# First mixture of a fused attention and two-mixture kernel: blocks of 256 tokens, rows fetched one expert ahead, gate weight kept in the row

## The chip, the cores and the metric

The kernel runs on one core of a Trainium2 chip. Its engines are TensorE (PE in the rows, PEld its weight loads, PEq and PEldq its sequencer), VectorE (DVE), ScalarE (ACT), GpSimd (POOL) and SyncE (SP, which here only issues transfers). Each engine runs its own instruction stream in order. The metric is the device time in microseconds; lower is better.

## The reference

```python
# attention: (B,H,S,D) = (4,8,576,64), softmax inside chunks of 64; then x = (2304, 512)
def _moe_ref(x, w_gate, w1, w2, capacity):        # first mixture: one expert per token
    logits = x @ w_gate                            # E = 8
    expert_idx = np.argmax(logits, axis=1)
    gate_w = softmax(logits)[arange(N), expert_idx]
    # the first `capacity` = 576 tokens of each expert are kept, in order of token
    h = np.maximum(disp[e] @ w1[e], 0.0)           # (tokens, 512) @ (512, 1024)
    y = h @ w2[e]                                  # (tokens, 1024) @ (1024, 512)
    out[i] = gate_w[i] * y[...] if kept else 0
def _moe2_ref(x, w_gate, w1, w2):                  # second mixture: every expert for every token
    P = exp(logits - max); 8 rounds of row and column normalisation
    out = sum over e of P[:, e] * (relu(x @ w1[e]) @ w2[e])
```

All matrix products of the mixtures are made in three fp16 products (high x high, high x low, low x high) that accumulate in PSUM.

## The kernel before

There are three stages. The first does attention and the routing, tile by tile of 128 tokens. It leaves in HBM the token rows `xs_d` (high and low fp16 halves side by side, 2 KB a row), their gate weights `kx_d` (one word a row), and on the chip the table `gidx`, which lists the tokens of each expert in groups of 128, and the counts `reg_i`. The second stage, the first mixture, is the one that changes. The third is the second mixture over all tokens, three quarters of the span.

The first mixture goes through the eight experts in a Python loop. `rc` is the expert's token count, loaded into a register of every engine (line 760), `rb` its first row in the output. `gather` (line 642) issues two indirect transfers on POOL, for the rows and for the gate weights. `turn` (line 653) transposes the rows by a transfer that SP issues. `block` (line 673) computes 128 tokens: the first layer of 8 x 12 matmuls of 128 columns (line 685) into PSUM in two groups of four, each group cut into a high half by ACT (line 688) and a low half by DVE (line 689); the second layer of 24 matmuls of 512 columns (line 697); scaling; and two writes by SP, of the rows (line 709) and of coefficient and token (line 715). Block 0 of an expert is always computed, its rows being fetched one expert ahead. Blocks 1 to 3 stand each under `tc.If(rc > 128 * t)` (line 807), which also fetches the next tile; a loop for whatever lies beyond four blocks stands under `tc.If(rc > 512)` (line 812) inside the last one. An engine whose branch is not taken jumps over the block's instructions.

The same engines prepare the weights two experts ahead. Every expert has 4 MB of fp32 weights, loaded by SP in pieces of 512 KB (`loads`, in `parts`, between the blocks). `w_stat` takes statistics (ACT for the first matrix, DVE for the second), `w_scale` reduces them over the partitions on POOL, and `w_split` rounds to a high half on ACT (line 212) and leaves a low half on DVE (line 213), in eight steps. These steps are run at `sites` between the parts of a block: 5 and 7 after the two groups of block 0, and the others in blocks 1 to 3, or in an `Else` where those are skipped. For the last matrix (the seventh expert prepares the first of the second mixture) the splits are replaced by twelve steps of `w_quad` (line 220): for each quarter POOL makes four sums into the one buffer `wsum`, and ACT and DVE round them (lines 237 and 238).

Before the first block, `rows0` is gathered straight away, the loads of the third expert's weights are issued, the second expert's weights are split, and `turn_first` transposes the first tile on TensorE (line 667).

Of the kernel before, what the change touches and what calls it, by code (L numbers as in the profile page):

```python
# [10 lines left out]
F16 = mybir.dt.float16  # L11
# [18 lines left out]
def kernel(ctx, tc, q, k, v, w_gate, w1, w2, capacity, w2_gate, w21, w22, out):  # L30
# [11 lines left out]
    NSTAT = 4  # L42
# [10 lines left out]
    xs_d = dram.tile([N, DM], F32, name="xs_d")  # L53
    kx_d = dram.tile([N, 1], F32, name="kx_d")
# [19 lines left out]
    def pow2_of_max(mx, n, log2, tag):  # L74
        m, s, inv = smw(tag + "m", [128, n]), smw(tag + "s", [128, n]), smw(tag + "i", [128, n])
# [90 lines left out]
    def w_scale(x, nm):  # L166
        m = mats[x, nm]
        if x > E:
            m.am = over_partitions(m.mx, {"a": 288, "b": 292}[nm], 4)
            return  # L170
        m.am = smw("wam" + nm, [128, 4])
        op = bass.bass_isa.ReduceOp.add if m.ssq else bass.bass_isa.ReduceOp.max
        nc.gpsimd.partition_all_reduce(out_ap=m.am, in_ap=m.mx, channels=128, reduce_op=op)

    def w_scale2(x, nm):
        m = mats[x, nm]
        mm = smw("wmm" + nm, [128, 1])
        nc.vector.tensor_reduce(out=mm, in_=m.am, axis=AX.X, op=ALU.add if m.ssq else ALU.max)
        if m.ssq:
            m.s, m.inv = smw("ws" + nm, [128, 1]), smw("wi" + nm, [128, 1])  # L180
            pow2_of_sumsq(mm, LF, small.tile([128, 1], I32, tag="wh", name="wh"), m.s, m.inv)
        else:
            m.s, m.inv = pow2_of_max(mm, 1, LW, "w" + nm)
        other = mats.get((x, {"a": "b", "b": "a"}[nm]))
        if hasattr(other, "inv"):
            iw = iws[x] = smw("iw", [128, 1])
            nc.vector.tensor_tensor(out=iw, in0=other.inv, in1=m.inv, op=ALU.mult)


    def w_slot(x, n):  # L190
        pool, tag = slots.get(x, (wpool, 4 * (x % 3 // 2))) if x < E else (wpool, 0)
        return pool.tile([128, 4096], F16, tag=f"s{tag + n}", name=f"w{x}_{n}")

# [65 lines left out]
    with ExitStack() as actx:  # L259
# [145 lines left out]
        def st_lo(i):  # L405
# [3 lines left out]
            (nc.gpsimd if i < NT - 3 else nc.sync).dma_start(out=xs_d[i * 128:(i + 1) * 128, :], in_=hl.bitcast(F32))  # L409
# [23 lines left out]
        def route(g):  # L433
# [109 lines left out]
            def r_out():  # L543
                nc.vector.tensor_tensor(out=t["kx"], in0=t["kx"], in1=GT[g]["inv"], op=ALU.mult)
                (nc.gpsimd if g < NG - 1 else nc.sync).dma_start(out=kx_d[g * G * 128:(g + 1) * G * 128, :].rearrange("(j p) o -> p (j o)", p=128), in_=t["kx"])
# [84 lines left out]
    with ExitStack() as cctx:  # L630
# [5 lines left out]
        first = wpool.tile([128, 4096], F16, tag="s7", name="first")  # L636
# [5 lines left out]
        def gather(idx, tag, xg=None):  # L642
            if xg is None:
                xg = cp.tile([128, DM], F32, tag="xg" + tag, name="xg")
# [5 lines left out]
            return idx, kg, xg  # L650


        def turn(pre, tag):
            idx, kg, xg = pre
            xT = cp.tile([128, 2 * KD, 128], F16, tag="xT" + tag, name="xT")
            nc.sync.dma_start_transpose(out=xT, in_=xg.bitcast(F16))
            return idx, kg, xT

        def gather_t(idx, tag):
            return turn(gather(idx, tag), tag)  # L660

        def turn_first(pre):
            idx, kg, xg = pre
            xT = first[:, 1024:2048].rearrange("p (k n) -> p k n", n=128)
            p = ps_c.tile([128, 2 * KD, 128], F16, tag="y1", name="p_t")
            for kk in range(2 * KD):
                nc.tensor.transpose(p[:, kk, :], xg.bitcast(F16)[:, kk * 128:(kk + 1) * 128], id16)
            nc.scalar.copy(out=xT[:, 0:KD], in_=p[:, 0:KD])
            nc.vector.tensor_copy(xT[:, KD:2 * KD], p[:, KD:2 * KD])
            return idx, kg, xT  # L670


        def block(x, pre, row0, tag, sites=((), (), ())):
            a, b = mats[x, "a"], mats[x, "b"]
            idx, kg, xT = pre
            hh = cp.tile([128, KF, 128], F16, tag="hh" + tag, name="hh", bufs=1)
            hl = cp.tile([128, KF, 128], F16, tag="hl" + tag, name="hl", bufs=1)
            for fg in range(KF // 4):
                p = ps_c.tile([128, 4, 128], F32, tag="p" + tag, name="p_h")
                for f4 in range(4):  # L680
                    f = fg * 4 + f4
                    n = 0
                    for w, lo in ((a.hi, 0), (a.hi, KD), (a.lo, 0)):
                        for kk in range(KD):
                            nc.tensor.matmul(p[:, f4, :], lhsT=w[:, kk, f * 128:(f + 1) * 128], rhs=xT[:, lo + kk, :],  # L685
                                             start=(n == 0), stop=(n == 3 * KD - 1))
                            n += 1
                nc.scalar.activation(out=hh[:, fg * 4:fg * 4 + 4, :], in_=p, func=AF.Relu)  # L688
                nc.vector.scalar_tensor_tensor(out=hl[:, fg * 4:fg * 4 + 4, :], in0=p, scalar=0.0,  # L689
                                               in1=hh[:, fg * 4:fg * 4 + 4, :], op0=ALU.max, op1=ALU.subtract)  # L690
                for f in sites[fg]:
                    f()
            y = ps_c.tile([128, DM], F32, tag="y" + tag, name="p_y")
            n = 0
            for kk in range(KF):
                for h, w in ((hh, b.hi), (hh, b.lo), (hl, b.hi)):
                    nc.tensor.matmul(y, lhsT=h[:, kk, :], rhs=w[:, kk, :], start=(n == 0), stop=(n == 3 * KF - 1))  # L697
                    n += 1
            sq, ssq = cp.tile([128, DM], BF16, tag="sq" + tag, name="sq2", bufs=1), sm("ssq2" + tag, [128, 1])
            nc.scalar.activation(out=sq, in_=y, func=AF.Square, accum_out=ssq)  # L700
            s, inv = sm("x2s" + tag, [128, 1]), sm("x2i" + tag, [128, 1])
            pow2_of_sumsq(ssq, LX, sm("x2h" + tag, [128, 1], I32), s, inv)

            rhl = cp.tile([128, 2, 2, DM // 2], F16, tag="row" + tag, name="row2", bufs=1)
            yh = y.rearrange("p (c n) -> p c n", c=2)
            nc.scalar.activation(out=rhl[:, :, 0, :], in_=yh, func=AF.Copy, scale=s)
            nc.vector.scalar_tensor_tensor(out=rhl[:, :, 1, :], in0=yh, scalar=s, in1=rhl[:, :, 0, :],
                                           op0=ALU.mult, op1=ALU.subtract)
            nc.sync.dma_start(out=x2_d[bass.ds(row0, 128), :],
                              in_=rhl.rearrange("p c l n -> p (c l n)").bitcast(F32))  # L710
            to = sm("rkt" + tag, [128, 2])
            nc.gpsimd.tensor_copy(to[:, 1:2].bitcast(I32), idx)
            nc.vector.scalar_tensor_tensor(out=to[:, 0:1], in0=kg, scalar=inv, in1=iws[x],
                                           op0=ALU.mult, op1=ALU.mult)
# [475 lines left out]
```

## Time and profile before

| | us |
|---|---|
| median of 3 runs | 1937.91 (1935.62 to 1939.22) |
| the profiled execution | 1938.3 |
| its span, first to last instruction | 1936.6 |
| TensorE busy in the span | 1780.1 |
| mean granted TensorE clock | 0.96 of full speed |

The profile's times are microseconds from the span's start. Busy time is the union of an engine's instructions; matmuls overlap, so the mean of one is longer than its share of the time. In a row of the timeline the two first numbers are start and length, `xN` counts merged instructions, and the bracket gives the idle time of that engine before them and what ended it.

### The profile page before, as it was taken

To read this page: it belongs to the slowest core of one execution; us is meant where nothing else is said; L and a number is where in the kernel's file an instruction comes from. 1 tells how busy PE (TensorE), PEld (TensorE's weight loads), DVE (VectorE), ACT (ScalarE), POOL (GpSimd) and SP (SyncE) were. 2 spreads that over 40 slices of the span, in tenths; PEclk is the share of its full clock that TensorE was granted. 3 is DMA by queue.
4 is the path that set the end of the run, shared out by engine and by line. 5 is a ranking of instruction groups with operands and counts; after the bars stand their busy time and mean duration, and the time that the engine had idled before them with its cause. 6 is when DMAs were issued, how large, how long until landed. Compare 5 with 4: busy or idle time off the path is not lost.

```text
span 1936.6 us, 28661 instructions
## 1 busy us (share of the span) xinstructions
PE 1780.1 (92%) x11303; PEld 1022.2 (53%) x11303; DVE 1016.2 (52%) x1960; ACT 708.9 (37%) x1283; POOL 429.0 (22%) x504
## 2 busy tenths in 40 slices
PE   7864868767999899999999999999999999999997
PEld 5753556545554445555555555555555555555553
DVE  5886465563656663464445345544545553465432
ACT  7954354453433333343323224312333332242210
POOL 1252021232110321041122113210311231042221
PEclk9976889888999899999999999999999999999999
DMA  9974666764414120222121121302311211211210
GB/s 224 189 155 132 178 178 146 156 162 91 139 66 128 58 96 6 101 80 79 58 78 67 58 94 64 101 18 84 101 58 58 101 44 57 101 58 63 78 39 33
DMA packets 146523, 182.91 MB, mean 94 GB/s; under 512 B 74352, under 2 KB 92784, under 8 KB 146352
## 3 DMA queue, kind: packets, MB, share of 16 engines
q1 hardware_dynamic: 139584, 165.09, 30.0%
q0 software_dynamic: 5712, 15.49, 2.9%
q8 instruction: 109, 1.79, 0.4%
q14 instruction: 62, 0.51, 0.1%
q10 hardware_dynamic: 1056, 0.03, 0.0%
HBM read 147.52 MB, written 22.97 MB: 88 GB/s over the span
## 4 chain that ended last, share of the span: by engine, by line
PE 67%; DVE 4%; ACT 3%; issue 1%; POOL 1%; DMA 0%; POOLq 0%; DVEq 0%
PE p_m L1075 38%; PE p_m L1013 28%; DVE c L1019 1%; DVE el L1030 1%; ACT eh L1029 1%; ACT wsq L154 1%; POOL w L1048 1%; PE p_m L903 0%; PE p_l L163 0%; ACT m L1038 0%; ACT m L1058 0%; DVE w L213 0%; DVE u L1019 0%; ACT w L212 0%; DMA out_dram<-acc,rk 0%
## 5 line engine op out<-in xcount | busy, mean ns | idle before, releaser
L1075 PE MATMUL p_m<-w,eh 128*128 128x512 f16 x2304 | 685.4, 379 | 0.6 <-ACT eh L1029 0.6
L1013 PE MATMUL p_m<-x,w 128*128 128x384 f16 x4032 | 667.7, 327 | 1.3 <-DVE c L1019 1.3
L1013 PEld LDWEIGHTS <-w 128*128 128x128 f16 x4032 | 396.2, 99 | 265.0 <-issue 6.8
L1075 PE MATMUL p_m<-w,el 128*128 128x512 f16 x1152 | 436.6, 379 | 0.0
L1075 PEld LDWEIGHTS <-eh 128*128 128x128 f16 x2304 | 225.4, 98 | 267.8 <-ACT eh L1029 1.1
L1029 ACT ACTIVATE eh<-c 128x384 f16<-128x384 f32 x384 | 190.5, 518 | 413.4 <-DVE c L1019 413.2
L1048 POOL TENSOR_TENSOR w<-u,m 128x384 f32<-128x384 f32 x96 | 96.6, 1006 | 991.0 <-DVE u L1019 913.5
L1147 DVE SCALAR_TENSOR_TENSOR acc<-p_m,cf,acc 128x512 f32<-128x512 f32 x126 | 94.6, 751 | 383.2 <-PE p_m L1075 377.0
L1030 DVE SCALAR_TENSOR_TENSOR el<-c,eh 128x384 f16<-128x384 f32 x384 | 217.9, 569 | 127.0 <-ACT eh L1029 116.5
L1038 ACT COPY m<-p_m 128x384 f32<-128x384 f32 x96 | 44.6, 465 | 399.6 <-PE p_m L1013 399.6
L1075 PEld LDWEIGHTS <-el 128*128 128x128 f16 x1152 | 112.7, 98 | 136.5 <-DVE el L1030 0.8
L685 PE MATMUL p_h<-xT,w 128*128 128x128 f16 x1824 | 125.7, 239 | 55.6 <-PEq L807 26.4
L685 PEld LDWEIGHTS <-w 128*128 128x128 f16 x1920 | 130.9, 110 | 64.3 <-issue 48.6
L697 PE MATMUL p_y<-w,hh 128*128 128x512 f16 x320 | 98.3, 390 | 7.3 <-ACT hh L688 7.3
L1053 POOL TENSOR_TENSOR c<-u,m 128x384 f32<-128x384 f32 x96 | 95.7, 997 | 3.6 <-DVE u L1019 3.1
L1019 DVE TENSOR_TENSOR u<-p_m,m 128x384 f32<-128x384 f32 x96 | 53.4, 556 | 61.7 <-PE p_m L1013 61.7
L1019 DVE TENSOR_TENSOR c<-p_m,w 128x384 f32<-128x384 f32 x96 | 53.5, 557 | 49.4 <-PE p_m L1013 33.5
L237 ACT ACTIVATE w<-wsum,wsa 128x1024 f16<-128x1024 f32 x32 | 36.6, 1145 | 90.1 <-POOL wsum L231 90.1
L1019 DVE TENSOR_TENSOR u<-p_m,u 128x384 f32<-128x384 f32 x96 | 53.5, 557 | 28.7 <-PE p_m L1013 26.8
L154 ACT ACTIVATE wsq<-sta 128x1024 bf16<-128x1024 f32 x64 | 67.5, 1054 | 0.6
L238 DVE SCALAR_TENSOR_TENSOR w<-wsum,wsa,w 128x1024 f16<-128x1024 f32 x32 | 41.1, 1283 | 46.8 <-ACT w L237 46.8
L697 PE MATMUL p_y<-w,hl 128*128 128x512 f16 x160 | 62.6, 391 | 2.7 <-DVE hl L689 2.7
(226 smaller groups left out, 1564.8 us busy)
## 6 DMA issues: line engine op xcount, KB each, us to landing
x<-xt_d SPq DMA_DIRECT2D x147, 384.0 KB, 4.5
sta<-in_moe_w_dram SPq DMA_DIRECT2D x18, 1024.0 KB, 7.0
stb<-in_moe_w_dram SPq DMA_DIRECT2D x18, 1024.0 KB, 7.6
sta<-in_moe_w_dram SPq DMA_DIRECT2D x28, 512.0 KB, 7.7
stb<-in_moe_w_dram SPq DMA_DIRECT2D x28, 512.0 KB, 8.5
xt_d<-x SPq DMA_DIRECT2D x21, 384.0 KB, 2.9
x_d<-row SPq DMA_DIRECT2D x20, 256.0 KB, 4.8
vbd<-in_v_dram SPq DMA_DIRECT2D x72, 64.0 KB, 4.5
```

Source lines behind the costliest of these rows:

```text
L154: nc.scalar.activation(out=sq, in_=src, func=AF.Square, accum_out=m.mx[:, h:h + 1])
L685: nc.tensor.matmul(p[:, f4, :], lhsT=w[:, kk, f * 128:(f + 1) * 128], rhs=xT[:, lo + kk, :], start=(n == 0), stop=(n == 3 * KD - 1))
L697: nc.tensor.matmul(y, lhsT=h[:, kk, :], rhs=w[:, kk, :], start=(n == 0), stop=(n == 3 * KF - 1))
L1013: nc.tensor.matmul(p, lhsT=wt[:, w, lw, kk, :], rhs=xt[:, lx, kk, :], start=(n == 0), stop=(n == 5))
L1019: nc.vector.tensor_tensor(out=c, in0=p, in1=t, op=ALU.add)
L1029: nc.scalar.activation(out=hh[:, sl], in_=src, func=AF.Relu)
L1030: nc.vector.scalar_tensor_tensor(out=hl[:, sl], in0=src, scalar=0.0, in1=hh[:, sl], op0=ALU.max, op1=ALU.subtract)
L1038: nc.scalar.copy(out=Q["m1"], in_=p)
L1048: nc.gpsimd.tensor_tensor(out=Q["w"], in0=Q["u2"], in1=Q["m5"], op=ALU.add)
L1053: nc.gpsimd.tensor_tensor(out=Q["c22"], in0=Q["u3"], in1=Q["m5"], op=ALU.add)
L1075: nc.tensor.matmul(y, lhsT=h[:, t * 128:(t + 1) * 128], rhs=w[:, kk, :], start=(n == 0), stop=(n == 3 * KF - 1))
L1147: nc.vector.scalar_tensor_tensor(out=acc[:, j, :], in0=y, scalar=coefs[x][:, j:j + 1], in1=acc[:, j, :], op0=ALU.mult, op1=ALU.add)
```

## The change

1. `xs_d` is made 8 words wider (520 words a row). The gate weight is written eight times over into these words, and `kx_d` goes; so one gather brings rows and gate weight, and `weights` copies the weight out of the gathered row on POOL.
2. `blocks` computes one or two tiles of 128 tokens in one first layer: the matmuls take 256 columns, PSUM groups hold two or four of the eight column blocks, in four buffers. The second layer still goes by tile.
3. An expert is now at most two such calls and the loop: tiles 0 and 1 under `tc.If(rc > 128)`, with an `Else` that computes tile 0 alone, then tiles 2 and 3 under `tc.If(rc > 256)` and `tc.If(rc > 384)`, with an `Else` for tile 2 alone. Tile 0 is no longer outside of the branches.
4. `fetch` gathers and transposes two tiles. Tiles 2 and 3 of an expert are fetched when the expert begins, tiles 0 and 1 of the next expert right after them, whether they hold tokens or not, and outside of the branches.
5. The steps of weight preparation go, all of them, into the first call (2, 2, 1 and 7 after the four groups, 5 after tile 0, the rest after tile 1; 3, 7 and the rest in the `Else`). The loads stand after the first and after the second call. At the stage's start the transposes of tiles 2 and 3 stand before the loads of the third expert.

```diff
+    XW = DM + 8
+    xs_d = dram.tile([N, XW], F32, name="xs_d")
-            (nc.gpsimd if i < NT - 3 else nc.sync).dma_start(out=xs_d[i * 128:(i + 1) * 128, :], in_=hl.bitcast(F32))
+            (nc.gpsimd if i < NT - 3 else nc.sync).dma_start(out=xs_d[i * 128:(i + 1) * 128, 0:DM], in_=hl.bitcast(F32))
...
+                wide = lambda a: a.unsqueeze(2).to_broadcast([128, G, XW - DM])
+                nc.vector.tensor_tensor(out=t["kx"], in0=wide(kx), in1=wide(GT[g]["inv"]), op=ALU.mult)
+                (nc.gpsimd if g < NG - 1 else nc.sync).dma_start(out=xs_d[g * G * 128:(g + 1) * G * 128, DM:XW].rearrange("(j p) o -> p j o", p=128), in_=t["kx"])
...
+        def gather(idx):
+            xg = cp.tile([128, XW], F32, tag="xg", name="xg", bufs=4)
             nc.gpsimd.indirect_dma_start(out=xg, out_offset=None, in_=xs_d[:, :],
                                          in_offset=bass.IndirectOffsetOnAxis(ap=idx, axis=0))
-            kg = cp.tile([128, 1], F32, tag="kg" + tag, name="kg", bufs=4)
-            nc.gpsimd.indirect_dma_start(out=kg, out_offset=None, in_=kx_d[:, :],
-                                         in_offset=bass.IndirectOffsetOnAxis(ap=idx, axis=0))
+            return idx, xg[:, DM:DM + 1], xg
+        def fetch(idxs, tag, bufs):
+            xT = cp.tile([128, 2 * KD, 128 * len(idxs)], F16, tag="xT" + tag, name="xT", bufs=bufs)
+            rows = []
+            for n, (idx, kg, xg) in enumerate([gather(idx) for idx in idxs]):
+                nc.sync.dma_start_transpose(out=xT[:, :, n * 128:(n + 1) * 128], in_=xg[:, 0:DM].bitcast(F16))
+                rows.append((idx, kg))
+            return xT, rows
+        def weights(pre):
+            xT, rows = pre
+            for n, (idx, kx) in enumerate(rows):
+                kg = cp.tile([128, 1], F32, tag="kg", name="kg", bufs=6)
+                nc.gpsimd.tensor_copy(kg, kx)
...
+        def blocks(x, pre, nb, row0, sites=()):
+            W = 128 * nb
+            FG = 512 // W
+            for fg in range(KF // FG):
+                p = ps_c.tile([128, FG, W], F32, tag="p", name="p_h", bufs=4)
+                for f4 in range(FG):
+                    for w, lo in ((a.hi, 0), (a.hi, KD), (a.lo, 0)):
+                        for kk in range(KD):
+                            nc.tensor.matmul(p[:, f4, :], lhsT=w[:, kk, f * 128:(f + 1) * 128], rhs=xT[:, lo + kk, 0:W],
...
+                site()
+            for t in range(nb):
+                y = ps_c.tile([128, DM], F32, tag="y", name="p_y", bufs=3)
...
+        rows0 = [gather(gidx[:, 0, t:t + 1]) for t in (0, 1)]
+        late = fetch([gidx[:, 0, t:t + 1] for t in (2, 3)], "c", 1)
...
+            cur = weights(pre)
+            if x > 0:
+                late = fetch([gidx[:, x, t:t + 1] for t in (2, 3)], "c", 1)
             if x + 1 < E:
+                pre = fetch([gidx[:, x + 1, t:t + 1] for t in (0, 1)], "m", 2)
...
+            with tc.If(rc > 128) as cmp:
+                blocks(x, cur, 2, rows(0), spread((2, 2, 1, 7, 5)))
+            with cmp.Else():
+                blocks(x, cur, 1, rows(0), spread((3, 7)))
+            for f in (loads(3, "a", 0, 4) if x == 0 else []) + (loads(x + 3, "b", 0, 4) if x != E - 3 else []):
+                f()
+            weights(late)
+            with tc.If(rc > 256):
+                with tc.If(rc > 384) as cmp:
+                    blocks(x, late, 2, rows(2))
+                    with tc.If(rc > 512):
+                        with tc.For_i(4, (rc + 127) // 128, 1) as t:
+                            idx = cp.tile([128, 1], I32, tag="idx", name="idx")
+                            nc.vector.tensor_copy(idx, gidx[:, x, bass.ds(t, 1)])
+                            blocks(x, weights(fetch([idx], "l", 1)), 1, lambda _: rank(t))
+                with cmp.Else():
+                    blocks(x, late, 1, rows(2))
+            for f in loads(E, "b", 0, 4) if x == E - 3 else loads(x + 4, "a", 0, 4):
+                f()
```

## Rows read from the trace of the kernel before

**Rows 1.** The page: busy time by engine, share of the span, instructions.

```profile
PE 1780.1 (92%) x11303; PEld 1022.2 (53%) x11303; DVE 1016.2 (52%) x1960; ACT 708.9 (37%) x1283; POOL 429.0 (22%) x504
```

**Rows 2.** The first mixture as one window: length, busy time of each engine, clock, DMA.

```profile
core 0: us, PE busy (x) PEld busy (x) DVE busy (x) ACT busy (x) POOL busy (x), PEclk, DMA share, GB/s
...
166.90:473.80 306.90, 241.08 (x2400) 176.77 (x2399) 173.64 (x313) 147.28 (x225) 75.84 (x102) 0.87 0.64 154
```

**Rows 3.** Windows of the eight experts, second-layer matmuls (line 697) alone.

```profile
166.90:228.50 61.60, 23.94 (x96) 9.65 (x96) 0.85 0.55 148
228.50:249.90 21.40, 5.34 (x24) 2.31 (x24) 0.85 0.55 167
249.90:308.00 58.10, 21.37 (x96) 9.24 (x96) 0.88 0.76 174
308.00:348.00 40.00, 16.03 (x72) 6.93 (x72) 0.96 0.65 158
348.00:381.20 33.20, 10.69 (x48) 4.62 (x48) 0.88 0.79 167
381.20:405.40 24.20, 5.34 (x24) 2.31 (x24) 0.71 0.89 199
405.40:450.50 45.10, 18.49 (x72) 7.17 (x72) 0.87 0.45 104
450.50:473.80 23.30, 10.69 (x48) 4.62 (x48) 0.93 0.54 138
```

**Rows 4.** TensorE's timeline, first expert: starts of two layers and the next.

```profile
212.35 0.59 PE L697 MATMUL p_y<-w,hh 128*128 128x512 f16 x2
...
217.53 5.52 PE L685 MATMUL p_h<-xT,w 128*128 128x128 f16 x96
222.89 0.59 PE L697 MATMUL p_y<-w,hh 128*128 128x512 f16 x2
```

**Rows 5.** TensorE's timeline, layers that began after idle time.

```profile
231.99 6.64 PE L685 MATMUL p_h<-xT,w 128*128 128x128 f16 x87 [2.33 <-issue]
...
250.26 3.25 PE L685 MATMUL p_h<-xT,w 128*128 128x128 f16 x29 [6.44 <-PEq L807]
258.82 6.28 PE L685 MATMUL p_h<-xT,w 128*128 128x128 f16 x67 [5.31 <-issue]
...
363.67 8.36 PE L685 MATMUL p_h<-xT,w 128*128 128x128 f16 x96 [4.67 <-DMA xT<-xg]
...
430.60 0.61 PE L697 MATMUL p_y<-w,hh 128*128 128x512 f16 x2 [3.92 <-ACT hh L688]
```

**Rows 6.** Waits from 160 to 482 us: total, times, longest.

```profile
PE p_h L685 <- PEq L807: 26.4, 5, 11.0
...
PE p_h L685 <- DMA xT<-xg: 14.7, 4, 6.6
```

**Rows 7.** Branches on TensorE's queue (min/median/max ns): two lines, then 243 to 252 us.

```profile
L807 PEldq COMPARE_BRANCH  x34: 73/178/5293, 183.6 to 473.9; - x34
...
L812 PEldq COMPARE_BRANCH  x4: 176/258/343, 224.5 to 307.7; - x4
...
L807 PEldq COMPARE_BRANCH  x2: 822/2748/4674, 244.0 to 245.0; - x2
```

**Rows 8.** Timeline of all engines at the start of the first mixture.

```profile
152.95 1.76 SPq L143 DMA_DIRECT2D sta<-in_moe_w_dram  x4
...
159.15 0.96 POOL L648 DMA_INDIRECT kg<-kx_d,gidx  x1 [4.35 <-DMA kx_d<-gkx]
165.26 1.03 PE L667 MATMUL p_t<-id,first 128*128 128x128 f16 x8 [15.73 <-DMA first<-xs_d,gidx]
```

**Rows 9.** Groups by shape in the first mixture: busy us, mean ns, idle before.

```profile
L685 PEld LDWEIGHTS <-w 128*128 128x128 f16 x1919 | 130.7, 110 | 64.3 <-issue 48.6 <-DMA xT<-xg 6.2 <-DVE w L213 4.7
...
L238 DVE SCALAR_TENSOR_TENSOR w<-wsum,wsa,w 128x1024 f16<-128x1024 f32 x4 | 5.1, 1281 | 10.8 <-ACT w L237 10.8
...
L230 POOL TENSOR_TENSOR wsum<-sta 128x256 f32<-128x256 f32 x4 | 2.9, 720 | 0.0
```

**Rows 10.** The page's DMA issues: median us from issue to landing.

```profile
xT<-xg SPq DMA_TRANSPOSE x25, 7.1
```

More of the change, by code (lines that the diff above doesn't have):

```diff
@@ L41 @@
     scale = 1.0 / math.sqrt(D)
-    NSTAT = 4
     G = 3
@@ L653, in turn @@
[L653 to L670, printed above, removed]
@@ new lines, in turn_first @@
+        def turn_first(pres):
+            xT = cp.tile([128, 2 * KD, 256], F16, tag="xTm", name="xT", bufs=2)
+            for n, (idx, kg, xg) in enumerate(pres):
+                p = ps_c.tile([128, 2 * KD, 128], F16, tag="y", name="p_t", bufs=3)
+                for kk in range(2 * KD):
+                    nc.tensor.transpose(p[:, kk, :], xg[:, 0:DM].bitcast(F16)[:, kk * 128:(kk + 1) * 128], id16)
+                sl = slice(n * 128, (n + 1) * 128)
+                nc.scalar.copy(out=xT[:, 0:KD, sl], in_=p[:, 0:KD])
+                nc.vector.tensor_copy(xT[:, KD:2 * KD, sl], p[:, KD:2 * KD])
+            return xT, [(idx, kg) for idx, kg, _ in pres]
@@ new lines, in blocks, with site @@
+        def blocks(x, pre, nb, row0, sites=()):
+            a, b = mats[x, "a"], mats[x, "b"]
+            xT, rows = pre
+            W = 128 * nb
+            sites = list(sites)
+            def site():
+                for f in (sites.pop(0) if sites else ()):
+                    f()
+            hh = cp.tile([128, KF, 256], F16, tag="hh", name="hh", bufs=1)[:, :, 0:W]
+            hl = cp.tile([128, KF, 256], F16, tag="hl", name="hl", bufs=1)[:, :, 0:W]
+            FG = 512 // W
+            for fg in range(KF // FG):
+                p = ps_c.tile([128, FG, W], F32, tag="p", name="p_h", bufs=4)
+                for f4 in range(FG):
+                    f = fg * FG + f4
@@ L689, in block @@
[L689 to L714, printed above, removed]
@@ L719, in each @@
+            while sites:
+                site()
         def each(f, x, nm, n, *args):
@@ L762 @@
             y = x + 2
+            steps = []
+            if y <= E:
+                for nm in "ab":
+                    w_keep(y, nm)
             if y < E:
@@ L798, in rank, with rows @@
                                           skip_runtime_bounds_check_because="a block starts before the last token")
-            def rest(lo):
-                with tc.For_i(lo, (rc + 127) // 128, 1) as t:
-                    idx = cp.tile([128, 1], I32, tag="idx", name="idx")
-                    nc.vector.tensor_copy(idx, gidx[:, x, bass.ds(t, 1)])
-                    block(x, gather_t(idx, "1"), rank(t), "1")
-            for t in range(1, NSTAT):
-                with tc.If(rc > 128 * t) as cmp:
-                    if t + 1 < NSTAT:
-                        pre[t + 1] = gather_t(gidx[:, x, t + 1:t + 2], "1")
-                    block(x, pre[t], rank(t), "1", sites[t])
-                    if t + 1 == NSTAT:
-                        with tc.If(rc > 128 * NSTAT):
-                            rest(NSTAT)
-                            if x == E - 1:
-                                heads()
-                if any(sites[t]):
-                    with cmp.Else():
-                        for fs in sites[t]:
-                            for f in fs:
-                                f()
-                for f in parts[2 * t + 1]:
-                    f()
+            def rows(t0):
+                return lambda t: rb if t0 + t == 0 else rank(t0 + t)
```

114 lines of the change are left out of this document (59 added, 55 removed).

## The prediction, made before the changed kernel was run

> **What bounds the kernel now.** I read the page's busy line first, to see whether TensorE is the limit: 1780.1 of 1936.6 us busy [rows 1]. That average hides one stage. Cut by stretches, the first mixture runs from 166.9 to 473.8 us, 306.9 us, with TensorE busy 241.1 and a granted clock of 0.87, between its two levels of 1.2 and 2.4 GHz [rows 2]; what follows, 1936.6 - 473.8 = 1462.8 us, the change does not touch. Third, the stretches of the eight experts: 24 second-layer matmuls are one block, so the rows show 4, 1, 4, 3, 2, 1, 3 and 2 blocks, 20 in all [rows 3]. Fourth, TensorE's timeline, for what a block costs when nothing waits: the second layer from 212.35 to 217.53, 5.18 us; the first layer's 96 matmuls from 217.53 to 222.89, 5.36 us, 55.8 ns each [rows 4]. So 20 blocks are 20 x 10.54 = 210.8 us of work, and 306.9 - 210.8 = 96.1 us are lost. By expert, length less blocks x 10.54: 19.4, 10.9, 15.9, 8.4, 12.1, 13.7, 13.5, 2.2. This is all there is to win.
>
> Fifth, what the losses are. The first layer waits 14.7 us in four places for the transposed rows, and 26.4 us in five for TensorE's sequencer at the `If` of line 807 [rows 6]. Nothing computes there: the sequencer is at a branch. Of the 34 branches at that line the middle one takes 178 ns and the longest 5293 ns; those of line 812, which jump over one block, at most 343 ns; after the second expert, where three bodies are skipped in a row, two took 822 and 4674 ns [rows 7]. So a jump over one block is cheap, one that goes further can cost 4 to 5 us, and TensorE then waits again inside its matmuls, for nothing that the profile shows: 2.33 us after 9 matmuls, 5.31 us after 29 [rows 5]. Idle time costs twice. After 4.67 us of it the next first layer takes 8.36 us where the full pace takes 5.52 [rows 4, 5]: 2.8 us more.
>
> **Wider matmuls.** Eight pairs (2+2+1+1+1+1) and four single blocks replace 20 blocks. A first layer of 128 columns already runs at 128/2.4 = 53.3 ns plus 2.5, with the weight load hidden; 256 columns are then 106.7 + 2.5 = 109.2 ns, 10.5 us a pair against 10.7. Eight pairs save 2 us, so the work is 208.6 us. The Trainium skill (TensorE: Matmul & The Clock Gate, section Back-to-back issue gap) gives about 81 ns as the sustained distance of such pairs of load and matmul at 128 columns. The trace disagrees: 55.8 ns. By the page the 768 weight loads that fall away would be worth some 25 ns each, an estimate of 19 us more.
>
> **Rows outside the branches.** The four waits for transposes, 14.7 us [rows 6], and the slow matmuls after them are in no term of the sum below: I take them as gone, since each transpose is now issued at least one pair, 21 us, before its use. But three of the tiles that waited are the first after a pair, and there a new branch stands instead.
>
> **Branches.** This is the dear part. Before, a skipped tile is one `If`; TensorE jumps 1, 3, 1, 1, 2, 3, 1, 2 times per expert. After, each pair's `If` has an `Else` with the whole block over again, and the `For` too lies on the way: a full expert jumps over the `Else`, over the loop and over the other `Else` (3), each other expert jumps twice; 18 against 14. Prices: a single far jump after which work is still queued, 3.0 us on average (26.4 less 6.4 and 11.0 leaves 9.0 for three) [rows 5, 6]; I take 2.3, as TensorE runs into it with 20 us of queued pair. A near jump between bounds of nothing (hidden behind queued work, 0.34 us) and 0.8 + 2.3 = 3.1 us [rows 5, 7]: 2.0, since row and pattern show both stalls. Near and far in a row, 4.7 (the 4674 ns). Three in a row, 6.4 to 11.0 + post-stall [rows 5, 6]: 9. Exits and middles so:
> first expert: middle 2.0, exit into a one-block expert 9 (loop, `Else`, and the next `If` falls to its `Else`);
> second: exit 2.3; third: middle 2.0, exit 3.5 (two near ones, bounds 0.7 and 6); fourth: middle 4.7, no jump at its end; fifth: exit 9.5; sixth: 2.3; seventh: middle 4.7, no jump at its end; eighth as before.
> Sum 40.0 us, near the 26.4 plus stalls of now. To it the clock: 2.4 after the two long ones, 2.2 after the two of 4.7, 1.7 after three of 2 to 3.5, 0.8 after the short middles, 15.9.
> The Trainium skill says the same of the mechanism (Runtime: NRT & Kernel Launch, section Instruction fetch mechanics): a taken branch outside the window of fetched instructions must fetch before going on, so branches should be few. It speaks against this change, which adds four; that is the second rival.
>
> **Start of the stage.** The gate weight now lies in the row, so the first gather reads what the last gate write wrote. Today the small gather waits for that write until 159.15 us, while the big one had left before it [rows 8]; now both wait. Against that, 4 MB of weights for the third expert no longer run ahead of it: they are issued behind the transposes of tiles 3 and 4. Today's first transpose starts at 165.26, 6.1 us after 159.15 [rows 8]. Two gathers of 1 us (the small one takes 0.96), at most those 6.1 us to land and 16 transposes at 1.03 us for eight [rows 8] give a first matmul between 166 and 169; I take 168.4, 1.5 us later than now (166.9). The weights, issued at 152.95 today [rows 8], come some 17 us later, at 170; eight pieces then land until about 192, if 4 MB take the 20 us that they take at the stage's 154 to 200 GB/s [rows 2, 3]. ACT and DVE take their statistics between the groups of the first pair, in order, so the groups' outputs queue behind a load that is not there yet. Bounds: nothing, and 11 us, if the second layer waits from 181 to 192; I take 8.2, 2.8 of it the slow start of a first layer after idle time.
>
> **What hides the rest.** Four PSUM banks for the first layer hold a whole pair's groups, so 10 us of lag of ACT and DVE (eight splits of 1.28 us [rows 9]) pass under TensorE; without that cover each pair would pay up to 10. POOL gives up one of two gathers per tile; 32 tiles instead of 26 are gathered and transposed, 7.1 us median to landing [rows 10], a whole expert ahead: hidden, except for the third expert's second pair, whose transposes queue behind 4 MB of weights: 2.0, bounds nothing and 8. The late splits also cost 1 us in the first expert and 1.5 in the third.
> In the seventh expert all twelve quarter steps now follow the first pair. Their chain is serial, as one sum buffer serves all: POOL 4 x 0.72, DVE 1.28 [rows 9] and between them ACT, which I put at 1.1 as DVE's pass over the same tile takes 1.28: 5.3 us a quarter, 21 in all, while TensorE has 5 us (y of the second tile) + 5.4 (first layer of the third) + a branch. Today the same chain shows as 3.92 us before a second layer [rows 5]. Now the third tile waits some 10 us (21 less 5, 5.4 and part of the branch), and 2.6 more at the slow clock, of which 2.2 are counted above. Bounds 0 and 14. Late next is nothing: the last expert's weights are ready.
>
> **Sum.** Work 208.6; branches 40.0; clock 15.9; start of the first pair 8.2; splits 2.5; late transposes 2.0; quarters 10.4; 0.5 at the end. 288.1 us against 306.9: 18.8 less, plus 1.5 for the start: 17.3. The profiled execution took 1938.3 us, 0.4 more than the median, 1937.9. 1938.3 - 17.3 = 1921.0; I say 1922.
>
> **Rivals.** First, the chain of quarters and the late weights are milder than I think: 18 of the 21 us for them (8.2, 2.5, 10.4) vanish, 1904. For it: DVE and ACT are under 60% busy in the stage [rows 2]. Against: they are strictly in order. Chance 0.19.
> Second, slower: branches dearer. If a near jump is no longer cheap, because the code beyond a pair's longer body is never there in time, every jump costs 4.7 us, exposed: the two short middles rise by 2.7 and 1.5 of clock each, the third's exit by 5.9, the second's and sixth's by 2.4 each, the long exits by 5.1 and 4.6, the long middles by 4.7 each. Together 38 us, 1959; half of it is 1940. It decides from 1.1 us more per jump on (17.3 over the 16 ahead of the last expert). For it: 4674 and 5293 ns [rows 7]. Against: 343 ns. Chance 0.21.
> Third, nothing is won: the transposes stay late, as they share one queue with 2 MB loads; three of them late by 5 us, 1937. For it: 7.1 us to land [rows 10]. Against: they are issued a block of 21 us ahead. Chance 0.13.
> Fourth, a 128-column matmul does pay for its weight load. If the 110 ns of a load's record [rows 9] were its price, the 768 that fall away would each give 110 - 55.8 = 54 ns, 42 us, 1880. The full-pace rows [rows 4] speak against it. Chance 0.02. By the Trainium skill's figure above it would be 1903.
> My forecast itself has 0.45, and its own range is 1911 to 1934.
>
> **How the numbers follow.** No change means within 0.2%, 3.9 us: 1934 to 1942. Faster: 0.45 + 0.19 + 0.02 = 0.66; same 0.13; slower 0.21. The range leaves out the deep end of the first rival and the upper half of the second: 1900 to 1950.
>
> **What would show it.** The profile after should have no wait of the first layer for a transpose over 3 us; L685's successor with 96 matmuls of 256 columns in 10.5 us; stretches by expert of about 63, 16, 53, 40, 30, 15, 50 and 21 us; branches on TensorE's queue over 3 us at the ends of the first, second, fifth and sixth expert and in the middle of the fourth and seventh; a second layer in the seventh that waits some 10 us for ACT. I am wrong if the near jumps take microseconds, if the first pair waits over 9 us for ACT or DVE, or if the attention stage before 166.9 us moves, which I cost at nothing: its gate writes are as many, with eight equal words for one.

## The result and the profile after

The changed kernel took 1917.74 us (median of four, 1917.45 to 1919.09) against 1938.57 of the kernel before on the same chip: ratio 0.9897, 95% interval 0.988 to 0.9914, so 20.8 us faster. The forecast was 1922.0. Its profiled execution spans 1915.8 us, against 1936.6 before.

The total came out as forecast, its parts did not. The first first-layer matmul starts at 152.55 us, 14.4 us earlier than before; 1.5 later was forecast. From there to the last second-layer matmul, at 453.1, the stage takes 300.55 us, only 6.3 less than the 306.9 of [rows 2], where 18.8 less was forecast. Of the changed kernel, second-layer matmuls (now line 726), one window for each expert; columns as in [rows 2]:

```profile
152.55:208.99 56.44, 22.92 (x96) 9.60 (x96) 0.92 0.67 200
208.99:236.19 27.20, 5.34 (x24) 2.31 (x24) 0.69 1.01 208
236.19:283.39 47.20, 21.05 (x96) 9.38 (x96) 0.95 0.64 179
283.39:319.32 35.93, 15.89 (x72) 6.89 (x72) 1.00 0.79 161
319.32:350.00 30.68, 10.69 (x49) 4.70 (x48) 0.90 0.88 213
350.00:376.68 26.68, 5.34 (x24) 2.31 (x24) 0.76 1.00 240
376.68:432.12 55.44, 17.83 (x72) 7.30 (x72) 0.77 0.39 92
432.12:453.10 20.98, 10.66 (x49) 4.70 (x48) 1.00 0.50 139
```

Forecast were 63, 16, 53, 40, 30, 15, 50 and 21. The second and the sixth expert, which have one tile of 128 tokens each, are 11.2 and 11.7 us longer than that, and longer than in the kernel before too [rows 3]; the seventh is 5.4 us longer, while the first, third and fourth are 4 to 7 us shorter. TensorE's timeline shows where; these are first layers (line 711) and one second layer:

```profile
152.55 12.26 PE L711 MATMUL p_h<-xT,w 128*128 128x256 f16 x96 [0.67 <-ACT xT L686]
166.98 0.60 PE L726 MATMUL p_y<-w,hh 128*128 128x512 f16 x2 [2.17 <-ACT hh L715]
...
181.14 10.64 PE L711 MATMUL p_h<-xT,w 128*128 128x256 f16 x96
...
208.99 7.85 PE L711 MATMUL p_h<-xT,w 128*128 128x128 f16 x96 [6.85 <-issue]
236.19 13.10 PE L711 MATMUL p_h<-xT,w 128*128 128x256 f16 x96 [14.16 <-DVEq L835]
...
350.00 7.35 PE L711 MATMUL p_h<-xT,w 128*128 128x128 f16 x96 [9.68 <-DVEq L835]
376.68 12.83 PE L711 MATMUL p_h<-xT,w 128*128 128x256 f16 x96 [14.16 <-DVEq L835]
401.33 1.56 PE L711 MATMUL p_h<-xT,w 128*128 128x128 f16 x25 [1.46 <-issue]
406.03 6.91 PE L711 MATMUL p_h<-xT,w 128*128 128x128 f16 x71 [3.14 <-issue]
424.36 1.04 PE L726 MATMUL p_y<-w,hh 128*128 128x512 f16 x2 [11.42 <-ACT hh L715]
```

The first layer of a pair (two tiles in one call) needs at full pace 10.64 us for 96 matmuls (181.14), with no gap at the branch before it. After each one-tile expert, at 236.19 and 376.68, TensorE waits 14.16 us for DVE's sequencer at line 835, `If(rc > 256)`, and after the fifth expert, at 350.00, 9.68 us for the same. The 1.46 and 3.14 us at 401.33 and 406.03 are the middle of the seventh expert. The waits of TensorE in the stage, in total, count and longest, which answer to [rows 6]:

```profile
PE p_h L711 <- DVEq L835: 38.0, 3, 14.2
PE p_y L726 <- ACT hh L715: 14.1, 3, 11.4
PE p_h L711 <- issue: 11.5, 3, 6.9
```

Besides these, 2.9 us at the third expert's exit, 2.4 us for one of DVE's weight splits in the middle of the fourth and 3.5 us ahead of second layers for DVE's low halves. No wait for transposed rows is left (14.7 us in [rows 6]). The start of the stage, to compare with [rows 8]:

```profile
143.27 0.37 SPq L557 DMA_DIRECT2D xs_d<-gkr  x1
143.75 0.17 PE L637 MATMUL p_tab<-gohx,ones 128*128 128x16 f16 x1 [1.20 <-DVE gohx L636]
...
145.89 1.12 POOL L656 DMA_INDIRECT xg<-xs_d,gidx  x1 [3.68 <-DMA xs_d<-gkr]
...
149.55 1.01 PE L684 MATMUL p_t<-id,xg 128*128 128x128 f16 x8 [5.63 <-DMA xg<-xs_d,gidx]
...
155.87 1.78 SPq L144 DMA_DIRECT2D sta<-in_moe_w_dram  x4
```

The last gate write, issued at 143.27, has landed by 145.89, 2.6 us later, so the gathers leave ahead of the weight loads and their rows are there 3.7 us later. Before, the count matmul that ends the routing came at 149.36, 5.6 us later than here: part of the gain is made in the attention stage.

### The profile page after: what moved, and what is told of

Its sections match the earlier page's. It is cut to its first block, busy times and chain, and to the rows that moved or that the text cites. A ratio compares the mean times of both kernels' runs of the same rounds, so it can differ in the third digit from the quotient of the medians.

```text
span 1915.8 us, 27034 instructions
## 1 busy us (share of the span) xinstructions
PE 1764.6 (92%) x10543; PEld 995.3 (52%) x10543; DVE 1011.8 (53%) x1961; ACT 707.4 (37%) x1284; POOL 413.0 (22%) x516
## 4 chain that ended last, share of the span: by engine, by line
PE 68%; DVE 4%; ACT 3%; issue 1%; POOL 1%; DMA 0%; POOLq 0%; DVEq 0%
PE p_m L1101 38%; PE p_m L1039 28%; DVE c L1045 1%; DVE el L1056 1%; ACT eh L1055 1%; ACT wsq L155 1%; POOL w L1074 1%; PE p_m L929 0%; PE p_l L164 0%; ACT m L1064 0%; ACT m L1084 0%; DVE w L223 0%; ACT w L222 0%; DMA out_dram<-acc,rk 0%; DVE u L1045 0%
## 5 line engine op out<-in xcount | busy, mean ns | idle before, releaser
L1039 PEld LDWEIGHTS <-w 128*128 128x128 f16 x4032 | 396.6, 99 | 266.0 <-issue 8.5
L711 PE MATMUL p_h<-xT,w 128*128 128x256 f16 (+1 forms) x1152 | 120.6, 273 | 55.4 <-DVEq L835 38.0
L711 PEld LDWEIGHTS <-w 128*128 128x128 f16 x1152 | 106.7, 107 | 71.4 <-DVEq L835 39.4
L726 PE MATMUL p_y<-w,hh 128*128 128x512 f16 x320 | 97.8, 388 | 14.1 <-ACT hh L715 14.1
L223 DVE SCALAR_TENSOR_TENSOR w<-stb,wsb,w 128x1024 f16<-128x1024 f32 x60 | 75.3, 1278 | 6.4 <-ACT w L222 6.4
```

The lines of the kernel that those rows point to most:

```text
L223: nc.vector.scalar_tensor_tensor(out=m.lo[:, sl, :], in0=m.st[:, sl, :], scalar=m.s, in1=m.hi[:, sl, :], op0=ALU.mult, op1=ALU.subtract)
L726: nc.tensor.matmul(y, lhsT=h[:, kk, sl], rhs=w[:, kk, :], start=(n == 0), stop=(n == 3 * KF - 1))
L1039: nc.tensor.matmul(p, lhsT=wt[:, w, lw, kk, :], rhs=xt[:, lx, kk, :], start=(n == 0), stop=(n == 5))
```

## The experiments

Every ratio is to the kernel before in the same run, from five rounds; the changed kernel stands at 0.9897.

### The same kernel again

> The changed kernel once more, to stand on one chip beside the next three and to show what of its trace repeats. If the early end of the routing belongs to the change, its last count matmul comes at 143 to 145 us again (149.36 in the trace of before) and the waits at the entries of the third and seventh expert are again near 14.2 us; if they were chance of one execution, they move by more than 2 us. Ratio to the kernel before 0.988 to 0.992.

0.9892 (0.9875 to 0.9909). Last count matmul at 143.65, first first-layer matmul at 152.32, both waits 14.16 us. All of these repeat.

### The start: gate weight in the row, and the width of its write

In the kernel before, with the gate weight moved into the row and nothing else of the change:

```
-    xs_d = dram.tile([N, DM], F32, name="xs_d")
-    kx_d = dram.tile([N, 1], F32, name="kx_d")
+    XW = DM + 8
+    xs_d = dram.tile([N, XW], F32, name="xs_d")
...
-            nc.gpsimd.indirect_dma_start(out=kg, out_offset=None, in_=kx_d[:, :],
-                                         in_offset=bass.IndirectOffsetOnAxis(ap=idx, axis=0))
...
+            nc.gpsimd.tensor_copy(kg, kx)
...
```

> The kernel before with one part of the change alone: the gate weight lies at the end of each row, written 32 bytes wide, and comes with the row's gather. Theory: the stage's early start comes from this part (the write lands in under 4 us instead of 10, so the first gather leaves before the weight loads); the first first-layer matmul goes from 166.96 to 153 to 157 us and the time is 1925 to 1930 us, all of it from the start. Rival: the early start comes from the rest of the change or from the attention stage by chance; then the first matmul stays at 165 us or later and the time is 1935 to 1941 us.

0.9956 (0.9941 to 0.9972), 8.5 us: as the theory had it. First first-layer matmul at 154.66, last count matmul at 144.07. So some 8.5 of the change's 20.8 us belong to the gate weight, if it adds to the rest of the change, which no run took by itself.

The kernel before, its own gate tensor kept, but eight words wide:

```
-    kx_d = dram.tile([N, 1], F32, name="kx_d")
+    kx_d = dram.tile([N, 8], F32, name="kx_d")
...
-            kg = cp.tile([128, 1], F32, tag="kg" + tag, name="kg", bufs=4)
+            kg = cp.tile([128, 8], F32, tag="kg" + tag, name="kg", bufs=4)
...
```

> The kernel before, gate weight still in a tensor of its own with a gather of its own, but 32 bytes wide instead of 4. If it is the width of the write that makes it land late (10 to 11 us for 384 pieces of 4 bytes), the writes land in 2 to 4 us here too, the first gather leaves near 147 us, the first first-layer matmul comes at 153 to 158 us, and the time is within 4 us of that of the kernel with the weight in the row (1925 to 1932 us). If it is the second gather and its wait that cost the time, the first matmul stays within 3 us of 166.96 and the time is 1935 to 1941 us.

0.9971 (0.9958 to 0.9985), 5.6 us. The first layer comes even earlier than expected and then waits:

```profile
142.81 0.17 PE L627 MATMUL p_tab<-gohx,ones 128*128 128x16 f16 x1 [1.26 <-DVE gohx L626]
...
148.59 8.19 PE L687 MATMUL p_h<-first,w 128*128 128x128 f16 x96 [0.67 <-ACT first L670]
165.70 1.03 PE L699 MATMUL p_y<-w,hh 128*128 128x512 f16 x2 [8.91 <-ACT hh L690]
```

The second layer starts at 165.70 here, at 166.95 with the weight in the row and at 166.98 in the changed kernel. In the last, ACT works through the second expert's eight splits until 166.4 (two groups of 4.27 and 4.25 us from 158.02) ahead of the first relu. Counted from the end of the routing, the second layer comes 22.9 us later in both of these kernels and 23.2 in the changed one, though their first layers start 5.8, 10.6 and 8.8 us after it: within these bounds the first layer's start does not set the second's.

So far the width of the write looked like the cause. The last run takes it away again from the changed kernel:

```
-    XW = DM + 8
+    XW = DM + 1
...
```

> The changed kernel with one word of gate weight at the end of each row in place of eight (rows of 513 words). Theory: the width of the gate write gave most of the early start; with pieces of 4 bytes the writes land 10 us or more after their issue again, ACT waits for row buffers in the attention stage again, the last count matmul comes at 148 to 151 us and the first first-layer matmul at 162 to 172, and the ratio to the kernel before is 0.993 to 0.998. Rival: one gather per tile, or its place ahead of the weight loads, made the start early; then the routing still ends near 143.7, the first matmul comes before 156 and the ratio stays at 0.988 to 0.991.

0.9901 (0.9882 to 0.9921), 1918.21 us: the theory fell. Pieces of 4 bytes, now 2052 bytes apart, land in 3.9 us (median of the page's DMA issues), the routing ends at 144.54 and the first layer starts at 153.84. DMA in the stretch from 75 to 145 us, first the kernel before, then this one; packets, MB, and share of the time of 16 engines:

```profile
q1 hardware_dynamic: 11775, 7.86, 63.3%
```

```profile
q1 hardware_dynamic: 11933, 7.90, 37.9%
```

The same bytes in as many packets kept the engines busy for 63.3% of the time before. There the gate writes took 11.3 us to land, and ACT waited 6.5 us in two places for row buffers whose writes had not landed; the page has 8.4 us for SP's three row writes, against 2.8 in the changed kernel. In all thirteen other profiles of this study the count matmul that ends the routing comes between 142.40 and 145.20 us. What is special before is that 384 neighbouring words of a small tensor are written as pieces of 4 bytes. Neither half of that is slow by itself: pieces of 4 bytes in rows of 513 words are not, and neither are neighbouring pieces of 32 bytes in the tensor eight words wide (38.7% in the same stretch; the last write, issued at 142.27, has landed by 144.79). That the two together are slow fits the four layouts, but only one profile shows it, and how they would slow the engines is not shown. This stays open.

The Trainium skill (DMA: Bandwidth & Descriptors, section Specifications) says that transfers under 512 bytes cost a read, a change and a write back. That would treat 4 and 32 bytes alike; 11.3, 3.9 and 2.5 us for pieces that are all shorter show that size alone does not sort them.

### The exits of the one-tile experts

The eight splits left for after the output row go behind the skipped pair:

```
-                blocks(x, cur, 1, rows(0), spread((3, 7)))
+                blocks(x, cur, 1, rows(0), [steps[0:3], steps[3:10], steps[10:12]])
...
+            if steps[12:]:
+                with tc.If(rc <= 128):
+                    for f in steps[12:]:
+                        f()
```

> The changed kernel, but in an expert with one tile the eight weight splits that were left for after its output row are emitted behind the skipped pair instead of ahead of it. Theory: PE waits 14.16 us at the entry of the third and of the seventh expert because DVE reaches the skipped branch only after its eight splits of 1.28 us; then both waits fall to 3 to 5 us, up to 3 us each come back at the second layer, which now finds the hl work of the next expert behind the splits, and the kernel takes 1898 to 1905 us. Rival: the 14.16 us are the far jump itself (code that has to be fetched); then the waits stay within 2 us of 14 and the time is 1917 to 1921 us.

0.989 (0.9876 to 0.9905): not to be told from the changed kernel. The waits did get shorter, though not to the 3 to 5 us that were expected. First the changed kernel, then this one: DVE's last four splits, and TensorE after them.

```profile
231.21 4.86 DVE L223 SCALAR_TENSOR_TENSOR w<-stb,wsb,w 128x1024 f16<-128x1024 f32 x4
...
236.19 13.10 PE L711 MATMUL p_h<-xT,w 128*128 128x256 f16 x96 [14.16 <-DVEq L835]
```

```profile
230.60 4.87 DVE L223 SCALAR_TENSOR_TENSOR w<-stb,wsb,w 128x1024 f16<-128x1024 f32 x4
...
230.09 13.38 PE L711 MATMUL p_h<-xT,w 128*128 128x256 f16 x96 [8.73 <-DMA xT<-xg]
```

In the changed kernel TensorE starts 0.1 us after DVE's last split; with the splits behind the branch it starts while they still run. So it was not the jump alone, which is still made: DVE was what it waited for, and behind that stood the next pair's transposes, 5 us less late. At the seventh expert 10.86 us remain of 14.16, put down to SP's sequencer. In this one profiled execution the stage takes 294.20 us, 6.4 less than in the changed kernel; the ratio has 1.4 us less, and each of the two ratios is known to some 3 us. How much the deferral gives by itself is not settled.

Next, the order of the two fetches turned round (`pre` ahead of `late`), with the splits still deferred:

> The kernel with the splits deferred, and besides the fetch of the next expert's first pair ahead of the fetch of the expert's own late pair. With the splits deferred the third expert still began 8.73 us and the seventh 10.86 us after the expert before it. Theory: what is late then is the first pair's transposes, which SP issues behind the two of a late pair that a one-tile expert never reads; then these waits fall to 3 to 6 us, and the ratio to 0.983 to 0.986 (the deferral alone: 0.989). Rival: what is left is the far jump with the code behind it; then the waits stay within 2 us of 8.7 and 10.9 and the ratio within 0.0015 of 0.989.

0.9898 (0.9883 to 0.9913): nothing won. The third expert's wait is 5.21 us, but its own second pair, fetched later, then waits 5.68 (0.90 with the splits deferred alone); the seventh's wait is 11.41. In the first of the kernels under Together, where this part is the same code, the three are 9.15, 6.26 and 12.02: one execution tells the third expert's wait only to some 4 us, and what both show is the new wait of the second pair.

Then the late fetch left out where it is never read:

```
+            if x in (1, 5):
+                late = cur
-            if x > 0:
+            elif x > 0:
                 late = fetch([gidx[:, x, t:t + 1] for t in (2, 3)], "c", 1)
...
-            weights(late)
+            if late is not cur:
+                weights(late)
```

> The kernel with the splits deferred, and without the fetch of a late pair in the second and sixth expert, which have one tile for this input and never read it (two gathers and two transposes less in each; the branch and its code stay). Theory: after the splits, the entries of the third and seventh expert wait for the first pair's transposes, which start only when POOL and SP have come into the one-tile expert and stand behind the late pair's there; the waits fall from 8.73 and 10.86 us to 3 to 6 us, and the ratio from 0.989 to 0.983 to 0.987. Rival: the rest is the far jump; then the waits stay within 2 us and the ratio within 0.0015 of 0.989.

0.9851 (0.9826 to 0.9875), some 8 us less than the changed kernel, but not by the waits falling to 3 to 6 us: they are 7.79 and 12.07. From the one-tile expert's first matmul to the next expert's it took 27.20 and 26.68 us in the changed kernel, 21.98 and 23.73 with the splits deferred, and 19.87 and 24.03 here (in a stage of 290.63 us). By the traces most of the gain came with the deferral, by the times it came only now; how the two share it is not settled. At the seventh expert, SP and TensorE:

```profile
355.60 5.57 SPq L665 DMA_TRANSPOSE xT<-xg  x2
361.60 0.36 SPq L738 DMA_DIRECT2D x_d<-row  x1
362.23 0.34 SPq L744 DMA_DIRECT2D rk_d<-rkt  x1
```

```profile
364.76 13.53 PE L711 MATMUL p_h<-xT,w 128*128 128x256 f16 x96 [12.07 <-SPq L838]
```

SP issues the transposes and the rows in order, and only then reaches the branch whose skip TensorE waits for, 2.2 us before TensorE starts. Late is the fetch: POOL's second gather waits for SP and leaves 8 us after the one-tile expert began (340.73), so in an expert of 24 us "one expert ahead" is hardly ahead:

```profile
348.67 0.94 POOL L656 DMA_INDIRECT xg<-xs_d,gidx  x1 [9.62 <-SPq L838]
```

How the 2.2 us divide between SP's skip and TensorE's jump is not shown.

### The quarter steps of the seventh expert

```
                 steps = stats(E) + scales(E) + [lambda q=q, i=i: w_quad(E, q, i) for q, i in QUADS]
+                steps, kept = steps[:17], steps[17:]
...
             if x == E - 1:
-                steps = [early]
+                steps = [early] + kept
...
-                blocks(x, cur, 2, rows(0), spread((2, 2, 1, 7, 5)))
+                blocks(x, cur, 2, rows(0), spread((2, 2, 1, 7, 5) if x < E - 1 else (2, 2, 2, 2)))
```

> The changed kernel, but the last seven quarter steps of the seventh expert move into the first layer of the eighth. Theory: the third tile's second layer waits 11.42 us for ACT's relu because ACT stands behind those steps; the wait goes to under 1 us and, as the eighth expert has room on ACT and DVE, the kernel takes 1907 to 1911 us. Rival: the steps only move the wait, to the second layer of the eighth expert or to the start of the second mixture, which needs the quarters; then the time is 1914 to 1919 us.

0.9858 (0.9843 to 0.9872): 7.5 us less than the changed kernel, where 1907 to 1911 us meant 7 to 11 less. The wait of the second layer falls from 11.42 to 4.12 us, not to under 1, since three of the steps still stand ahead of the relu on ACT, and the seventh expert takes 43.56 instead of 55.44 us:

```profile
415.92 0.61 PE L726 MATMUL p_y<-w,hh 128*128 128x512 f16 x2 [4.12 <-ACT hh L715]
```

Of these 11.9 us, 3.6 are lost again in the earlier experts of this execution, whose code is the same. The wait does not come back later: the eighth expert's pair runs at 10.64 us.

### Width and early fetch by themselves

Two matmuls of 128 columns for each one of 256:

```
+                    for c in range(nb):
+                        cs = slice(c * 128, c * 128 + 128)
...
-                            nc.tensor.matmul(p[:, f4, :], lhsT=w[:, kk, f * 128:(f + 1) * 128], rhs=xT[:, lo + kk, 0:W],
...
+                                nc.tensor.matmul(p[:, f4, cs], lhsT=w[:, kk, f * 128:(f + 1) * 128], rhs=xT[:, lo + kk, cs],
...
```

> The changed kernel with two first-layer matmuls of 128 columns in place of one of 256. Theory: weight loads of 128 columns are hidden, 192 x 55.8 ns = 10.7 us against the 10.64 us measured for 96 x 256 columns, so the width gives nothing by itself and the time is within 3 us of the changed kernel (ratio 0.988 to 0.992). Rival: a matmul of 128 columns that needs a new weight each time costs more, 81 ns by the Trainium skill; then each of the eight pairs takes 4.9 us longer and the time is some 39 us above (ratio 1.008 to 1.012).

0.9944 (0.9929 to 0.9958), some 10 us above the changed kernel in the times, 3.5 in the span of its profiled execution, which was its fastest. The weight loads are hidden, as the theory had it, but the time is not within 3 us. A pair at full pace takes 10.88 us, 0.24 more:

```profile
180.47 10.88 PE L713 MATMUL p_h<-xT,w 128*128 128x128 f16 x192
```

That is 56.7 ns a matmul, 2 us over eight pairs. The other waits moved by a few us each (17.07 instead of 11.42 in the seventh expert), and where the rest of the 10 us arises is not settled. It is not in TensorE's work: its busy time in the stage is 226.0 us, against 228.2 and, in the second execution of the changed kernel, 226.3. The Trainium skill's 81 ns (TensorE: Matmul & The Clock Gate, section Back-to-back issue gap) does not hold for this stream: 56.7 ns.

The late pair's fetch back inside the branch that reads it:

```
-                late = fetch([gidx[:, x, t:t + 1] for t in (2, 3)], "c", 1)
...
             with tc.If(rc > 256):
+                late = weights(fetch([gidx[:, x, t:t + 1] for t in (2, 3)], "c", 1))
...
```

> The changed kernel with the late pair's fetch put back into the branch that reads it (the gathers of the two kinds of pair get two buffers each). Theory: fetched at the top of the expert, the late pairs come for nothing; in the branch each of the four experts with more than two tiles waits for a gather and two transposes, 8 to 14 us at the middle, while the one-tile experts lose the same two gathers and transposes that delayed their exits; together 20 to 50 us slower than the changed kernel (ratio 1.000 to 1.016). Rival: the transposes were hidden behind the first pair's tail anyway; then the middles stay under 3 us and the ratio is 0.984 to 0.992.

1.0307 (1.0285 to 1.0329): 59 us slower than before, 80 slower than the changed kernel. The theory had the right sign and too small a size. The waits of the first layer for transposes:

```profile
PE p_h L711 <- DMA xT<-xg: 99.3, 4, 28.4
```

Four waits of some 25 us: in the branch the gathers start when the pair is done, and queue behind the next expert's fetch and the weight loads. The kernel before also fetched inside its branches, but each of them the tile after its own; so these 80 us price a fetch at the moment of its use, not what the change saved.

### Together

Deferred splits, turned order and moved quarters:

> The deferred splits, the first pair fetched ahead of the late pair, and the last seven quarter steps in the eighth expert, together. If the three gains add, the ratio is 0.9795 to 0.983 (1894 to 1901 us against 1934); if the one-tile exits stay as they are, it is that of the moved quarters alone, 0.985 to 0.987.

0.9861 (0.9843 to 0.9879): the quarters' gain alone. Deferred splits, no idle late fetch and moved quarters:

> The same with the last seven quarter steps moved into the eighth expert as well. If the gains add, the ratio is 0.979 to 0.983; if the one-tile exits give nothing, it is that of the moved quarters alone, 0.985 to 0.987.

0.9798 (0.9778 to 0.9818), 1897.95 us: some 19 us less than the changed kernel and the fastest here, though for counts like these only, as it names the two one-tile experts. These take 17.40 and 23.48 us in its profile. The third expert waits 4.54 us at its entry and again, for transposes, 3.39 in its middle. From the first first-layer matmul to the last second-layer one:

```profile
153.98:437.00 283.02, 228.54 (x1632) 153.67 (x1631) 171.37 (x313) 145.01 (x223) 54.40 (x104) 0.90 0.71 176
```

17.5 us of the changed kernel's 300.55 are gone, with as much busy TensorE: 228.5 us against 228.2.

## Why the prediction was right, and where not

**Wider matmuls: right.** 10.64 us a pair at full pace (10.5 forecast), against 10.88 in two halves: 1.9 us over eight pairs, 2 forecast. That busy TensorE fell from 241.1 [rows 2] to 228.2 is not the width's doing, as it is 226.0 with the halves too. What fell is the time that matmuls take beyond full pace: 30.3 us before (241.1 less 210.8), 19.6 now (228.2 less 208.6), close to the 18.7 that the forecast gave to the clock (15.9, and 2.8 in the first pair).

**Rows ahead: right for the long experts.** All four waits for transposes [rows 6] are gone, as forecast, and a fetch at the moment of its use would cost 80 us. For the entries behind the one-tile experts it does not hold: with DVE's splits out of the way, late transposes or SP's queue are the next wait.

**Branches: 54.8 us for the forecast's 40.0, and wrong in the parts.** TensorE's waits ahead of and within first layers sum to 54.8 us (38.0 + 11.5 + 2.9 + 2.4). The middles of the first and third expert cost nothing (2.0 each forecast); the fourth's is 2.4, put down to a split of DVE's, and the seventh's 4.6 (4.7 each); the exits of the first and third 6.85 and 2.90 (9, 3.5). The step that failed is the exit of the second and sixth expert: "2.3" each, 14.16 measured, 23.7 us together. I read the waits of [rows 6] for TensorE's sequencer as jumps and priced the jump of TensorE alone. What it waits for is another engine's arrival at the same branch: DVE had eight splits in front of it, 9.7 us; the last ended at 236.07, and its first semaphore of line 835 came at 236.1. With the splits gone, SP's queue or the transposes come next.

```profile
L835 DVEq EVENT_SEMAPHORE  x4: 21/21/21, 236.1 to 456.0; - x4
```

The fifth's exit, 9.68 us, met its forecast of 9.5 for the wrong reason: there too DVE still had splits to do, the last three of them after the second tile's row.

```profile
345.77 0.21 DVE L742 SCALAR_TENSOR_TENSOR rkt<-kg,x2i,iw 128x1 f32<-128x1 f32 x1
346.14 3.68 DVE L223 SCALAR_TENSOR_TENSOR w<-stb,wsb,w 128x1024 f16<-128x1024 f32 x3 [0.16 <-ACT w L222]
```

They end at 349.82, and TensorE starts at 350.00. This is read from the trace alone: deferring the splits of pairs as well was not tried. The Trainium skill's rule on taken branches (Runtime: NRT & Kernel Launch, section Instruction fetch mechanics) fits the first expert's exit, where the profile shows no other cause: TensorE's branches at line 835 took up to 7.54 us. No run tests it, and in two other executions (moved quarters, turned order) that exit, 7.35 and 7.98 us, is put down to the landing of output rows.

**Start of the stage: wrong by 16 us.** The "at most those 6.1 us to land" began from 159.15, the landing of the gate write before, about 10 us after its issue. I took that for a property of the write; in the changed kernel it is 2.6 us at most. With it fell two other steps. The weights were not late: they are issued at 155.87 instead of 152.95, not at 170. And the attention stage, "which I cost at nothing" and named as a place where I might be wrong, ends 5.6 us earlier. The 8.2 us that the first pair was to lose came as 7.6 (181.14 - 152.55 less 10.64 + 2 x 5.18), but by another cause: the second expert's splits on ACT ahead of the second layer, not late weights; 4.1 of it are idle time, the rest slow matmuls. (4 MB at the 154 to 200 GB/s named there are 21 to 27 us, not the forecast's 20.)

**Quarters: right in mechanism and size.** 10.4 forecast, 11.42 measured (12.70 in the second execution), and 7.5 us came back when most of it was moved.

**The sum.** Inside the stage the gain fell 12.5 us short of the forecast (6.3 for 18.8); at its start it was 15.9 above (14.4 for -1.5). The two nearly cancel, and 1922 was close largely by luck. The stage's 300.55 us close as 228.2 busy, 54.8 at first layers and 17.6 ahead of second layers (14.1 and 3.5, where 8.2 less 2.8, 2.5 and 10.4 had been forecast, 18.3), so what fell short inside is in the main the branches' 14.8. What is not luck: work, clock, transposes and quarters.

## What to carry to other kernels

A skipped branch costs more than the jump: an engine with work left in front of it can hold up one that has none, so look at every engine's queue ahead of a branch, not at the jumping engine's alone. Work "one step ahead" is ahead by the length of the shortest step, and in that one it should be left out. Before you price a transfer as given, ask whether its time belongs to it or to how and where its pieces are written.

## What was not expected of the hardware

Pieces of 4 bytes to neighbouring words took 11.3 us to land in the kernel before, and SP's row writes 8.4 us instead of 2.8; pieces of 4 bytes 2052 bytes apart took 3.9 us, and pieces of 32 bytes 2.5; why is open. TensorE, at a branch that both skip, started 0.1 to 0.2 us after DVE's last instruction ahead of that branch.
